# Retention attention with a two-level router: scores on array quarters, router products beside the transposes, ranks behind the scores

## The chip, the cores and the metric

The kernel runs on one core of a Trainium2 chip. The metric is the device time of one execution in microseconds (us). An execution is one launch, from the inputs in the chip's main memory to the finished output there. Five engines work beside one another, each with its own queue of instructions in program order: TensorE (PE, with PEld for its weight loads), VectorE (DVE), ScalarE (ACT), GpSimd (POOL) and SyncE (SP), which here only starts transfers (DMAs).

## The reference

Two stages. The first is a linear attention with a decay for each of 8 heads; q, k and v have 4 sequences of 768 tokens and 64 features a head. The second sends each of the 3072 tokens (512 features) to one of four groups, and in it to one of four experts, of a two-layer network of 1024 hidden features.

```python
for t in range(S):
    state = gamma[None, :, None, None] * state + np.einsum('bhd,bhe->bhde', k[:, :, t], v[:, :, t])
    y[:, :, t] = scale * np.einsum('bhd,bhde->bhe', q[:, :, t], state)
...
g_logits = x @ w_group
g_idx = np.argmax(g_logits, axis=1)
...
        h = np.maximum(xg[mask_e] @ w1[g, e], 0.0)
        ye = h @ w2[g, e]
        combined = g_w[mask_g][mask_e] * e_w[mask_e]
        out[tok_idx] = combined[:, None] * ye
```

g_w and e_w are the softmax weights of the chosen group and of the chosen expert.

## The kernel before

**Attention (lines 856 to 920).** The 3072 tokens are cut into 24 chunks of 128, six to a sequence, and `attention` runs over them (`ch` is the chunk). Inside a chunk the sum over keys is made by products, across chunks by a state. In program order a chunk issues: `vprep(ch+2)` (POOL: v times a power of the decay), `state_out` (L260, query by state, on 64 by 64 quarters of the array), `value_out` (L273, masked scores by values, 128 by 64), `state_mm` (L236, keys by values into the state in PSUM), `out_x` (DVE, L285: the chunk's x, written as `xt` from two PSUM tiles `op`; a chunk takes both, so the next chunk's `state_out` can start only when they are read), `state_copy` (ACT), router steps, the load of q and k of chunk ch+5, `logits(ch-1)`, `keys_mm(ch+1)` (L193, four transposes; the last chunk of a sequence needs none, nor a state), `trans_mm(ch-1)` (L291, four transposes of x) with `x_store(ch-1)` to main memory, `score_mm(ch+2)` (L214), `score_mask(ch+2)` (DVE, L221, one for each half of the heads), more router steps, and `logits_mm(ch)`. The first chunk of a sequence has no `state_out`.

**Scores (L203 to L214).** Heads are in four pairs. For each pair the two heads use the upper and the lower 64 rows of the array at once. The weights are the 128 keys (64 rows by 128 columns), the 128 queries are streamed, and the mask then sets to zero the products of keys later than their query.

**Router logits.** They are made in two steps: `logits_mm` (L305) multiplies each 128-feature quarter of x with its part of the router's weights (20 columns padded to 32, four column strips at once), ACT copies the result (`logits_copy`, `ls`), and `logits` (L316) adds up the four quarters by a product with a 0/1 matrix (`C_SEL`), from where ACT copies 20 columns to `L`. Both results and the ranks below lie in one PSUM tile, `log`.

**Routing (`route`, L324 on).** Chunks are routed in groups: `BATCHES = [(0, 4), (4, 4), (8, 4), (12, 5), (17, 4), (21, 3)]` (first chunk, count). A group's work is a generator, of which `route_steps` takes 5 steps at a time (6 from chunk 16 on), three times a chunk: twelve steps of small DVE operations (m, d, q, m2, o, oh, sm, eg, se, u, w, the reciprocal), then a "wait" mark, then the rank products on TensorE (L387, L389) from `oh`, then r1 and `nb` (DVE reads the ranks), r2, sf and slot. Only the first of the three calls, right behind `out_x` and `state_copy`, passes `ranks=True` and may go past the mark. A group enters the list in the chunk that follows its last one. `enlist` then scatters each chunk's tokens to the experts' lists (`meta`) by POOL; `clear_lists` fills the lists once before.

**Experts 0 and 1.** They have fixed early lists (of the first 12 chunks: `ua`, `va`) and late lists (`ub`, `vb`). The weights of `ua` are loaded in 16 parts in chunks 2 to 17 and split in chunks 4 to 19 (ACT makes the fp16 part `wh`, POOL the rest `wl`, L600 and L601); `va` is loaded in chunks 18 to 21 and its eight splits are made in chunks 20 (0 on DVE, 1 on POOL), 21 (2), 22 (3, 4, 5) and after the attention (6, 7). The layers of `ua` are a generator too, `self.first`: its first 24 products stand ahead of chunk 23's `state_out` (place 0 of `beside`), the others between the steps that follow chunk 23.

**Behind the attention** come the last group's route, the layers of `ua`, the expert order (`order`, small DVE operations on one row), then `va`, `ub`, `vb` and the other 14 experts (`us`, by size), each with transposes of gathered x (`xtrans`, L641), a first layer (`hps`, L664), a second (`yps`, L692, L742, L744) and a scatter of the result (POOL, L795). While one expert is computed, the next one's weights are split on ACT and DVE and those of the one after are loaded on SP's queue.

Of the kernel before, what the change touches and what calls it, by code (L numbers as in the profile page):

```python
# [22 lines left out]
P = 128  # L23
NC = S // P
# [22 lines left out]
C_TRI, C_GV, C_GS, C_SEL = 0, 128, 176, 180  # L47
C_STRI, C_DESC, C_SEG, C_KP, C_WP, C_IT = 200, 328, 348, 367, 386, 405
C_END = C_IT + MAXI

# [10 lines left out]
def constants():  # L61
# [3 lines left out]
    c[:, C_TRI:C_TRI + P] = s[:, None] <= s[None, :]  # L65

    n = np.arange(NC)[None, :, None] * P + s[:, None, None] + 1.0
    c[:, C_GV:C_GV + NC * H] = (g ** -n).reshape(P, NC * H)
    c[:, C_SEL:C_SEL + 20] = s[:, None] % 32 == np.arange(20)[None, :]
# [22 lines left out]
class Kernel:  # L92
# [15 lines left out]
    def setup(self):  # L108
# [15 lines left out]
        self.wr = cp.tile([P, 4, 32], F32, name="wr")  # L124
        nc.vector.memset(self.wr, 0.0)
        nc.sync.dma_start(self.wr[:, :, 0:20], self.a_wr.rearrange("p (k e) -> p k e", k=4))
# [58 lines left out]
    def keys_mm(self, ch):  # L185

        nc, s = self.nc, self.st[ch]
        if ch % NC == NC - 1:
            return
        s["kt"] = kt = self.pp.tile([P, 512], F32, name="kt", tag="big", bufs=3)  # L190
        for p in range(4):
            cs = slice(p * P, p * P + P)
            nc.tensor.transpose(kt[:, cs], s["ld"][:, DM + p * P:DM + p * P + P], self.ident)  # L193

    def keys_copy(self, ch):
        s = self.st[ch]
        if ch % NC == NC - 1:
            return
        s["kk"] = self.vp.tile([P, DM], F32, name="kk", bufs=2)
        self.nc.scalar.activation(s["kk"], s["kt"], AF.Copy)  # L200

    def score_mm(self, ch, pars=(0, 1)):


        nc, pp, s = self.nc, self.pp, self.st[ch]
        qT = s["ld"][:, 0:DM]
        kT = s["ld"][:, DM:2 * DM]
        for par in pars:
            s["sc", par] = pp.tile([P, 512], F32, name="sc", tag="big", bufs=3)
        for p in range(4):  # L210
            for par in pars:
                rs = slice(64 * par, 64 * par + 64)
                cs = slice(p * P, p * P + P)
                nc.tensor.matmul(s["sc", par][:, cs], kT[rs, cs], qT[rs, cs], start=True, stop=True)  # L214

    def score_mask(self, ch, par):
# [3 lines left out]
        tri = self.cst[:, C_TRI:C_TRI + P].unsqueeze(1).broadcast_to([P, 4, P])  # L220
        nc.vector.tensor_tensor(s["pf"][:, par], s["sc", par].rearrange("p (g t) -> p g t", g=4), tri, ALU.mult)  # L221
# [65 lines left out]
    def trans_mm(self, ch):  # L287
        nc, s = self.nc, self.st[ch]
        s["tp"] = self.pp.tile([P, 512], F32, name="tp", tag="tra", bufs=1)
        for j in range(4):  # L290
            nc.tensor.transpose(s["tp"][:, j * P:j * P + P], s["xt"][:, j, :], self.ident)  # L291

# [7 lines left out]
    def logits_mm(self, ch):  # L300

        nc, s = self.nc, self.st[ch]
        s["lt"] = lt = self.log[:, 256 + ch % 2 * P:256 + ch % 2 * P + P]
        for j in range(4):
            nc.tensor.matmul(lt[32 * j:32 * j + 32, :], self.wr[:, j, :], s["xt"][:, j, :], start=True, stop=True)  # L305

    def logits_copy(self, ch):
        s = self.st[ch]
        s["ls"] = self.wp.tile([P, P], F32, name="ls", bufs=2)
        self.nc.scalar.activation(s["ls"], s["lt"], AF.Copy)  # L310

    def logits(self, ch):

        nc, s = self.nc, self.st[ch]
        lg = self.log[:, ch % 2 * 64:ch % 2 * 64 + 20]
        nc.tensor.matmul(lg, s["ls"], self.cst[:, C_SEL:C_SEL + 20], start=True, stop=True)  # L316
# [4 lines left out]
        nc.scalar.activation(self.Ls[i][:, ch - c0, :], lg, AF.Copy)  # L321
# [530 lines left out]
    def attention(self, extra, beside):  # L852
# [20 lines left out]
        for ch in range(NCH):  # L873
# [7 lines left out]
            if ch == 6:  # L881
# [11 lines left out]
            self.route_steps(steps, True)  # L893
            if ch + 5 < NCH:
                self.load(ch + 5)
            if ch >= 1:
                self.logits(ch - 1)
# [3 lines left out]
            if ch >= 1:  # L901
                self.trans_mm(ch - 1)
                self.x_store(ch - 1)
# [9 lines left out]
            self.route_steps(steps)  # L913
# [3 lines left out]
            self.route_steps(steps)  # L917
            self.logits_mm(ch)
            self.logits_copy(ch)
            extra(ch)  # L920

    def route_steps(self, n, ranks=False):
# [4 lines left out]
        for i in range(n):  # L927
            if self.steps:
# [3 lines left out]
                if t == "wait" and not (ranks and i == 0):  # L932
# [3 lines left out]
    def run(self):  # L936
        tc, nc = self.tc, self.nc
        with ExitStack() as ctx:
# [29 lines left out]
            def extra(ch):  # L968
# [4 lines left out]
                if 18 <= ch <= 21:  # L973
                    self.wload(va, ch - 18)
# [3 lines left out]
                if ch == 20:  # L978
                    self.wsplit(va, 0)
                    self.wsplit(va, 1, eng=nc.gpsimd)  # L980
                if ch == 21:
                    self.wsplit(va, 2)
                if ch == NCH - 2:
                    for k in (3, 4, 5):
                        self.wsplit(va, k)
                    self.first = self.layers(ua)

            def beside(ch, place):
# [8 lines left out]
                if ch == NCH - 1 and place == 0:  # L997
                    first(2)
# [9 lines left out]
            first(1)  # L1008
            self.logits(last)
            assert not self.steps  # L1010
# [4 lines left out]
            first(1)  # L1015
            self.trans_mm(last)
            self.x_store(last)
            first(2)
# [38 lines left out]
            for i, k in enumerate(self.layers(ub)):  # L1057
                if k == 3:
# [84 lines left out]
```

## Time and profile before

| | us |
|---|---|
| median of 3 runs | 455.16 |
| lowest, highest | 452.87, 455.31 |
| the profiled execution | 459.31 |
| its span, first to last instruction | 457.6 |

| stretch of the span | PE busy | DVE busy | ACT busy | POOL busy | granted clock |
|---|---|---|---|---|---|
| 40 to 60 us (attention) | 18.88 of 20 | 13.87 | 9.69 | 12.53 | 1.00 |
| 100 to 120 us (attention, fourth group) | 15.72 of 20 | 10.71 | 6.64 | 9.79 | 0.83 |
| 120 to 140 us (last chunks) | 15.32 of 20 | 14.18 | 10.85 | 11.41 | 0.83 |
| 260 to 300 us (experts) | 39.79 of 40 | 31.41 | 24.69 | 15.96 | 1.00 |

The second table is from the view of busy time by windows. In rows of the timeline the columns are the start in us, the length in us, the engine, the line, the operation, the tiles (written <- read), the shape and the count; brackets give the idle time of the engine before it and what ended that. A TensorE row's length reaches to the modelled end of its last product, which overlaps the next row; so blocks are measured from start to start.

### The profile page before, as it was taken

How to read it: one execution, taken by the hardware profiler on the slowest of the kernel's cores; microseconds unless marked ns; L12 is line 12 of the kernel's file. 1: busy time of each engine (PE TensorE's matmuls, PEld its weight loads, DVE VectorE, ACT ScalarE, POOL GpSimd, SP SyncE). 2: the span in 40 equal slices, each digit the busy share in tenths (PEclk: the TensorE clock that was granted, in tenths of full speed). 3: DMA queues.
4: the chain of work that ended last, by engine and by line, in shares of the span. 5: the costliest groups of instructions: out<-in, count | busy, mean ns of one | idle time of the engine just before them, and what ended most of it. 6: DMA issues, size and time to landing. Idle time of an engine off the chain costs nothing.

```text
span 457.6 us, 12943 instructions
## 1 busy us (share of the span) xinstructions
PE 426.9 (93%) x5373; PEld 344.7 (75%) x5404; DVE 296.9 (65%) x499; ACT 233.0 (51%) x391; POOL 173.1 (38%) x148
## 2 busy tenths in 40 slices
PE   7998989987959899899999999999999999999991
PEld 4787878776848676677687978879789788788770
DVE  1448586565477626577679878677687687697720
ACT  1234445442545226455655656657666676676610
POOL 3714666655742622124150615336145044042011
PEclk9999999997988999999999999999999999999996
DMA  7878988885751295747766687787887887877000
GB/s 231 306 253 317 288 262 266 243 279 184 224 181 49 84 386 188 274 155 236 274 229 224 232 287 257 246 288 247 285 295 276 302 258 295 313 279 273 13 27 31
DMA packets 35055, 106.80 MB, mean 233 GB/s; under 512 B 13720, under 2 KB 14360, under 8 KB 27316
## 3 DMA queue, kind: packets, MB, share of 16 engines
q1 hardware_dynamic: 24052, 88.65, 57.3%
q0 software_dynamic: 10944, 17.31, 11.0%
q8 instruction: 43, 0.70, 0.6%
q14 instruction: 16, 0.13, 0.1%
HBM read 93.53 MB, written 13.77 MB: 234 GB/s over the span
## 4 chain that ended last, share of the span: by engine, by line
PE 58%; issue 24%; POOL 8%; DVE 5%; DMA 2%; SPq 1%; ACT 0%; POOLq 0%; DVEq 0%
PE hps L664 20%; PE yps L692 9%; PE yps L742 5%; PE yps L744 5%; PE sc L214 4%; PE op L273 4%; POOL out L795 3%; POOL xg L623 3%; PE tpx L641 2%; PE op L260 2%; PE tp L291 2%; PE kt L193 1%; PE stp L236 1%; PE log L305 1%; DMA ld<-qk 1%
## 5 line engine op out<-in xcount | busy, mean ns | idle before, releaser
L601 DVE TENSOR_TENSOR wl<-wf,wh 128x1024 bf16<-128x1024 f32 x119 | 144.0, 1220 | 40.8 <-ACT wh L600 34.5
L664 PE MATMUL hps<-xbh,wh 128*128 128x128 f16 (+14 forms) x576 | 135.4, 246 | 1.6 <-ACT xbh L643 0.8
L664 PE MATMUL hps<-xbl,wh 128*128 128x128 bf16 (+14 forms) x576 | 135.4, 246 | 1.1 <-issue 0.6
L664 PE MATMUL hps<-xbh,wl 128*128 128x128 f16 (+14 forms) x576 | 135.4, 246 | 0.9 <-issue 0.9
L600 ACT ACTIVATE wh<-wf 128x1024 f16<-128x1024 f32 (+1 forms) x136 | 133.9, 999 | 0.1
L795 POOL DMA_INDIRECT out<-yo,mt x32 | 41.4, 1294 | 192.8 <-ACT yo L760 170.5
L664 PEld LDWEIGHTS <-wh 128*128 128x128 f16 x1152 | 103.4, 98 | 5.7 <-issue 3.1
L669 ACT ACTIVATE hh<-hps 128x256 f16<-128x256 f32 (+14 forms) x72 | 35.0, 488 | 58.9 <-PE hps L664 52.4
L744 PEld LDWEIGHTS <-wh 128*128 128x128 f16 x704 | 44.6, 98 | 21.0
L664 PEld LDWEIGHTS <-wl 128*128 128x128 bf16 x576 | 56.7, 98 | 2.8 <-issue 2.2
L221 DVE TENSOR_TENSOR pf<-sc,cst 128x512 f32<-128x512 f32 x48 | 30.8, 684 | 41.3 <-PE sc L214 40.1
L623 POOL DMA_INDIRECT xg<-xd,mt x32 | 51.8, 1619 | 13.5 <-issue 5.8
L672 DVE SCALAR_TENSOR_TENSOR hl<-hps,hh 128x256 bf16<-128x256 f32 (+14 forms) x70 | 38.5, 552 | 22.5 <-ACT hh L669 21.0
L643 ACT ACTIVATE xbh<-tpx 128x512 f16<-128x512 f32 (+13 forms) x32 | 16.9, 527 | 45.1 <-PE tpx L641 45.0
L425 POOL DMA_INDIRECT meta<-src,slot x24 | 24.5, 1022 | 25.5 <-DVE rows L415 8.9
L644 DVE TENSOR_TENSOR xbl<-tpx,xbh 128x512 bf16<-128x512 f32 (+13 forms) x32 | 19.3, 602 | 22.7 <-ACT xbh L643 22.6
L742 PE MATMUL yps<-wh,hh 128*128 128x512 f16 x88 | 33.4, 380 | 0.0
L742 PE MATMUL yps<-wh,hl 128*128 128x512 f16 x88 | 33.4, 379 | 0.0
L214 PE MATMUL sc<-ld 64*128 64x128 f32 x384 | 30.5, 302 | 1.9 <-DMA ld<-qk 1.9
L601 POOL TENSOR_TENSOR wl<-wf,wh 128x512 bf16<-128x512 f32 (+1 forms) x17 | 20.7, 1220 | 29.7 <-ACT wh L600 26.3
L744 PEld LDWEIGHTS <-wl 128*128 128x128 bf16 x352 | 23.1, 98 | 10.4
L214 PEld LDWEIGHTS sc<-ld 64*128 64x128 f32 x384 | 25.6, 203 | 6.8 <-issue 5.6
(138 smaller groups left out, 658.6 us busy)
## 6 DMA issues: line engine op xcount, KB each, us to landing
wf<-w1p SPq DMA_DIRECT2D x28, 1024.0 KB
wf<-w2p SPq DMA_DIRECT2D x28, 1024.0 KB
ld<-qk SPq DMA_DIRECT2D x23, 512.0 KB
xd<-xr SPq DMA_DIRECT2D x24, 256.0 KB
vt<-vb SPq DMA_DIRECT2D x6, 768.0 KB
wf<-w1p SPq DMA_DIRECT2D x8, 256.0 KB
wf<-w2p SPq DMA_DIRECT2D x8, 256.0 KB
wf<-w1p POOLq DMA_DIRECT2D x2, 1024.0 KB
```

The source lines that it names most:

```text
L214: nc.tensor.matmul(s["sc", par][:, cs], kT[rs, cs], qT[rs, cs], start=True, stop=True)
L221: nc.vector.tensor_tensor(s["pf"][:, par], s["sc", par].rearrange("p (g t) -> p g t", g=4), tri, ALU.mult)
L600: nc.scalar.activation(u["wh"][i][:, cs], u["wf"][i][:, cs], AF.Copy)
L601: (eng or nc.vector).tensor_tensor(u["wl"][i][:, cs], u["wf"][i][:, cs], u["wh"][i][:, cs], ALU.subtract)
L623: nc.gpsimd.indirect_dma_start(out=xg[0:r, i, :], out_offset=None, in_=self.xd[0:n, :], in_offset=bass.IndirectOffsetOnAxis(ap=mt[0:r, i, ...
L664: nc.tensor.matmul(hv[:, a, 0:W], l[:, k, fs], r[:, k, 0:W], start=(n == 0), stop=(n == 11))
L669: nc.scalar.activation(hh[:, f, 0:W], hv[:, :, 0:W], AF.Relu)
L672: nc.vector.scalar_tensor_tensor(*rest)
L692: nc.tensor.matmul(ps[0:r, :], l[:, k, ts], m[k], start=(n == 0), stop=(n == 23))
L742: nc.tensor.matmul(big, h[:, k, 0:P], w[k], start=(n == 0), stop=(n == 23))
L744: nc.tensor.matmul(yv[:, d, 0:r], w[k][:, d * P:d * P + P], h[:, k, P:P + r], start=(n == 0 and d == 0), stop=(n == 23), skip_group_check= ...
L795: s = nc.gpsimd.indirect_dma_start(out=self.out, out_offset=bass.IndirectOffsetOnAxis(ap=mt[0:r, i, 0:1].bitcast(U32), axis=0), in_=yo[0:r ...
```

## The change

Five things are changed.

1. *Scores on quarters.* Each product of 128 keys by 128 queries is cut in two on 64 by 64 quarters: the earlier 64 keys by all 128 queries, and the later 64 keys by the later 64 queries. The quarter of later keys by earlier queries is not computed; the mask's zeros stand over it. Two PSUM tiles, cleared once by DVE, take the scores of all chunks. So that both column halves of the array get as much work, every other pair of heads has its keys in swapped halves (`KEYS`); keys, values, decays and the mask follow in the packing.
2. *Router products.* One step: four products with x as the weights (128 by 128) and the router's 20 columns streamed, added up in PSUM, right behind the transposes of x in `trans_mm`. The copy `ls`, the 0/1 matrix and its product go.
3. *Ranks.* The first call of `route_steps` in a chunk no longer goes past the mark, the two behind the scores and masks do; every mark now ends a call.
4. *Splits and loads.* `clear_lists` stands in chunk 4, the loads of `va` in 17 to 20, its splits 0, 1 and 2 on DVE in 19, 20 and 21; 3 stands ahead of `order`, 4 to 7 behind it. POOL clears the second gather buffer in place of DVE.
5. *Around the end of the attention.* The first 24 products of `ua` stand behind chunk 23. During `vb`, the transposes of the next expert's x stand at steps 8 and 10, its splits at 3, 7, 9, 11 and 13.

```diff
-C_TRI, C_GV, C_GS, C_SEL = 0, 128, 176, 180
+C_TRI, C_GV, C_GS, C_STRI, C_DESC = 0, 256, 304, 308, 436
+KEYS = np.array([np.arange(P) ^ (64 * (h // 2 % 2)) for h in range(H)])
...
+        self.sc = [self.pp.tile([P, 512], F32, name=f"sc{par}", tag="big", bufs=3) for par in range(2)]
+        self.kt = self.pp.tile([P, 512], F32, name="kt", tag="big", bufs=3)
+        for sc in self.sc:
+            nc.vector.memset(sc, 0.0)
...
         for p in range(4):
-            for par in pars:
-                rs = slice(64 * par, 64 * par + 64)
-                cs = slice(p * P, p * P + P)
-                nc.tensor.matmul(s["sc", par][:, cs], kT[rs, cs], qT[rs, cs], start=True, stop=True)
+            for late in range(2):
+                for par in range(2):
+                    half = (late + p) % 2
+                    rs = slice(64 * par, 64 * par + 64)
+                    ks = p * P + 64 * half
+                    cs = slice(p * P + 64 * late, p * P + P)
+                    nc.tensor.matmul(
+                        self.sc[par][64 * half:64 * half + 64, cs], kT[rs, ks:ks + 64], qT[rs, cs],
+                        start=True, stop=True, skip_group_check=True,
+                    )
...
+        for j in range(4):
+            nc.tensor.matmul(self.log[:, 0:20], s["xt"][:, j, :], self.wr[:, j, :], start=(j == 0), stop=(j == 3))
...
-            nc.tensor.matmul(lt[32 * j:32 * j + 32, :], self.wr[:, j, :], s["xt"][:, j, :], start=True, stop=True)
-
-    def logits_copy(self, ch):
-        s = self.st[ch]
-        s["ls"] = self.wp.tile([P, P], F32, name="ls", bufs=2)
-        self.nc.scalar.activation(s["ls"], s["lt"], AF.Copy)
...
-        nc.tensor.matmul(lg, s["ls"], self.cst[:, C_SEL:C_SEL + 20], start=True, stop=True)
...
-            if ch == 6:
+            if ch == 4:
                 self.clear_lists()
...
-            self.route_steps(steps, True)
+            self.route_steps(steps)
...
             if ch >= 1:
                 self.trans_mm(ch - 1)
+                self.logits(ch - 1)
                 self.x_store(ch - 1)
...
-            self.route_steps(steps)
+            self.route_steps(steps, True)
...
-            self.route_steps(steps)
-            self.logits_mm(ch)
-            self.logits_copy(ch)
+            self.route_steps(steps, True)
...
-                if t == "wait" and not (ranks and i == 0):
+                if t == "wait":
                     self.waiting = True
                     break
...
-                if 18 <= ch <= 21:
-                    self.wload(va, ch - 18)
+                if 17 <= ch <= 20:
+                    self.wload(va, ch - 17)
...
-                if ch == 20:
-                    self.wsplit(va, 0)
-                    self.wsplit(va, 1, eng=nc.gpsimd)
-                if ch == 21:
-                    self.wsplit(va, 2)
+                if 19 <= ch <= 21:
+                    self.wsplit(va, ch - 19)
                 if ch == NCH - 2:
-                    for k in (3, 4, 5):
-                        self.wsplit(va, k)
                     self.first = self.layers(ua)
...
-                if ch == NCH - 1 and place == 0:
-                    first(2)
...
-            first(1)
+            first(2)
+            self.trans_mm(last)
             self.logits(last)
+            self.x_store(last)
...
-            first(1)
-            self.trans_mm(last)
-            self.x_store(last)
-            first(2)
+            first(4)
...
+            nc.gpsimd.memset(self.xg[1], 0.0)
+            self.wsplit(va, 3)
             self.steps.append(self.order())
             self.route_steps(99)
             assert not self.steps
-            nc.vector.memset(self.xg[1], 0.0)
-            self.wsplit(va, 6)
-            self.wsplit(va, 7)
+            for k in range(4, 8):
+                self.wsplit(va, k)
...
             for i, k in enumerate(self.layers(vb)):
-                if k in KX:
-                    self.xtrans(us[0], ("tra", "sta")[KX.index(k)], (KX.index(k),))
-                if k is not None and k < 5:
-                    self.wsplit(us[0], k + 3)
-                    if k % 2 == 0:
-                        self.wload(us[1], k // 2 + 1)
+                if i in (8, 10):
+                    self.xtrans(us[0], ("tra", "sta")[i // 2 - 4], (i // 2 - 4,))
+                if i in (3, 7, 9, 11, 13):
+                    j = (3, 7, 9, 11, 13).index(i) + 3
+                    self.wsplit(us[0], j)
+                    if j % 2:
+                        self.wload(us[1], j // 2)
```

More of the change, by code (lines that the diff above doesn't have):

```diff
@@ L64, in constants @@
     c = np.zeros((P, C_END), np.float64)
-    c[:, C_TRI:C_TRI + P] = s[:, None] <= s[None, :]
-    n = np.arange(NC)[None, :, None] * P + s[:, None, None] + 1.0
+    for i in range(2):
+        c[:, C_TRI + i * P:C_TRI + i * P + P] = (s ^ (64 * i))[:, None] <= s[None, :]
+    n = np.arange(NC)[None, :, None] * P + KEYS.T[:, None, :] + 1.0
     c[:, C_GV:C_GV + NC * H] = (g ** -n).reshape(P, NC * H)
-    c[:, C_SEL:C_SEL + 20] = s[:, None] % 32 == np.arange(20)[None, :]
     for half in range(2):
@@ L189, in keys_mm @@
             return
-        s["kt"] = kt = self.pp.tile([P, 512], F32, name="kt", tag="big", bufs=3)
         for p in range(4):
             cs = slice(p * P, p * P + P)
-            nc.tensor.transpose(kt[:, cs], s["ld"][:, DM + p * P:DM + p * P + P], self.ident)
+            nc.tensor.transpose(self.kt[:, cs], s["ld"][:, DM + p * P:DM + p * P + P], self.ident)
     def keys_copy(self, ch):
@@ L219, in score_mask @@
             s["pf"] = self.wp.tile([P, 2, 4, P], F32, name="pf", bufs=3)
-        tri = self.cst[:, C_TRI:C_TRI + P].unsqueeze(1).broadcast_to([P, 4, P])
-        nc.vector.tensor_tensor(s["pf"][:, par], s["sc", par].rearrange("p (g t) -> p g t", g=4), tri, ALU.mult)
+        tri = self.cst[:, C_TRI:C_TRI + 2 * P].unsqueeze(1).broadcast_to([P, 2, 2 * P])
+        o, i = s["pf"][:, par].rearrange("p g t -> p (g t)"), self.sc[par]
+        o, i = (t.rearrange("p (i t) -> p i t", i=2) for t in (o, i))
+        nc.vector.tensor_tensor(o, i, tri, ALU.mult)
     def state_mm(self, ch):
@@ L320, in logits @@
             self.Ls[i] = self.rp.tile([P, BM, 20], F32, name="L", bufs=2)
-        nc.scalar.activation(self.Ls[i][:, ch - c0, :], lg, AF.Copy)
+        self.nc.scalar.activation(self.Ls[i][:, ch - c0, :], self.log[:, 0:20], AF.Copy)
     def route(self, i):
@@ L926, in route_steps @@
         self.waiting = False
-        for i in range(n):
+        for _ in range(n):
             if self.steps:
@@ L1057, in run @@
             for i, k in enumerate(self.layers(ub)):
-                if k == 3:
+                if i == 7:
                     self.xtrans(vb)
@@ L1114, in tokm, with keyed @@
         return a.reshape(B, H, NC, P, D).transpose(0, 2, 3, 1, 4).reshape(B, NC, P, DM)
+    def keyed(a):
+        a = a.reshape(B, H, NC, P, D)
+        return np.stack([a[:, h][:, :, KEYS[h]] for h in range(H)], axis=1).reshape(B, H, S, D)
     rows = np.concatenate([h * D + np.arange(D) for g in HEAD for h in g])
-    qk = np.concatenate([feat(q), feat(k)], axis=3).reshape(NCH, P, 2 * DM)
-    vb = tokm(v).reshape(NCH // GR, GR, P, DM).transpose(0, 2, 1, 3).reshape(NCH // GR, P, GR * DM)
+    qk = np.concatenate([feat(q), feat(keyed(k))], axis=3).reshape(NCH, P, 2 * DM)
+    vb = tokm(keyed(v)).reshape(NCH // GR, GR, P, DM).transpose(0, 2, 1, 3).reshape(NCH // GR, P, GR * DM)
     wr = np.concatenate([inp["moe_w_group"], inp["moe_w_expert"].transpose(1, 0, 2).reshape(DM, NX)], axis=1)
```

23 lines of the change are left out of this document (6 added, 17 removed).

## The prediction, made before the changed kernel was run

> **What bounds the kernel now.** I read the page first: who is busy, and when.
>
> ```profile
> span 457.6 us, 12943 instructions
> PE 426.9 (93%) x5373; PEld 344.7 (75%) x5404; DVE 296.9 (65%) x499; ACT 233.0 (51%) x391; POOL 173.1 (38%) x148
> ```
>
> TensorE is the bound. So time can be won in two ways: less TensorE work, or fewer of its gaps. Next the timeline of TensorE for one chunk of the attention stage; columns are start, length, line, tiles, count.
>
> ```profile
> 49.51 1.16 PE L214 MATMUL sc<-ld 64*128 64x128 f32 x16
> 50.60 0.42 PE L305 MATMUL log<-xt,wr 128*32 128x128 f32 x8
> 50.96 0.67 PE L260 MATMUL op<-ld,V 64*64 64x128 f32 x16
> 51.55 1.09 PE L273 MATMUL op<-pf,vs 128*64 128x128 f32 x16
> 52.48 0.64 PE L236 MATMUL stp<-vs,kk 128*64 128x64 f32 x16
> 53.04 0.40 PE L316 MATMUL log<-cst,ls 128*128 128x20 f32 x2
> 53.29 0.63 PE L193 MATMUL kt<-ident,ld 128*128 128x128 f32 x4
> 53.76 0.60 PE L291 MATMUL tp<-ident,xt 128*128 128x128 f32 x4
> 54.29 0.38 PE L214 MATMUL sc<-ld 64*128 64x128 f32 x2
> ```
>
> One chunk takes 54.29 - 49.51 = 4.78 us with TensorE never waiting. Start to start, the blocks cost: scores 1.09, router products 0.36, state output 0.59, value output 0.93, state 0.56, router sum 0.25, key transposes 0.47, x transposes 0.53. Then the same timeline where it does wait, at the fourth and fifth routing group.
>
> ```profile
> 17.32 1.09 PE L273 MATMUL op<-pf,vs 128*64 128x128 f32 x16
> ...
> 96.30 1.09 PE L273 MATMUL op<-pf,vs 128*64 128x128 f32 x16
> ...
> 100.02 1.09 PE L273 MATMUL op<-pf,vs 128*64 128x128 f32 x16
> ...
> 105.20 0.71 DVE L285 TENSOR_TENSOR xt<-op,gx 128x256 f32<-128x256 f32 x2
> ...
> 106.19 0.62 PE L316 MATMUL log<-cst,ls 128*128 128x20 f32 x2 [3.04 <-DVE nb L397]
> ```
>
> ```profile
> 124.67 1.16 PE L214 MATMUL sc<-ld 64*128 64x128 f32 x16
> 126.75 1.09 PE L273 MATMUL op<-pf,vs 128*64 128x128 f32 x16
> ...
> 132.73 0.40 PE L316 MATMUL log<-cst,ls 128*128 128x20 f32 x2 [2.75 <-DVE nb L397]
> ...
> 139.81 1.14 PE L273 MATMUL op<-pf,vs 128*64 128x128 f32 x16
> ```
>
> From value output 1 (17.32) to value output 22 (126.75) pass 109.4 us. Without waits it would be 15 full chunks of 4.78, three of 4.34 (the next chunk is a sequence's last, without the 0.47 of key transposes, less 0.03 that this had hidden) and three of 100.02 - 96.30 = 3.72 at the change of sequence: 95.9 us. So **13.5 us are waits**. The last step, 22 to 23, takes 13.06 us. I then asked for the windows around these gaps, cut where the granted clock changes (columns: window, length, PE busy, PEld, DVE, ACT, POOL, granted clock, DMA share, GB/s).
>
> ```profile
> 102.41:105.81 3.40, 0.34 (x6) 0.25 (x6) 3.23 (x10) 0.46 (x2) 2.16 (x2) 1.00 0.67 181
> 105.82:112.64 6.82, 6.45 (x54) 5.18 (x56) 2.21 (x8) 2.18 (x5) 2.44 (x3) 0.50 0.42 126
> 126.30:129.71 3.41, 2.04 (x49) 1.73 (x46) 3.24 (x11) 1.05 (x3) 1.79 (x2) 1.00 0.91 276
> 129.72:133.12 3.40, 0.65 (x9) 0.55 (x9) 3.22 (x13) 0.70 (x2) 0.00 (x0) 1.00 0.50 201
> 133.13:139.94 6.81, 6.25 (x58) 4.88 (x59) 4.03 (x5) 4.88 (x8) 4.33 (x4) 0.50 0.11 39
> ```
>
> A window with 0.34 or 0.65 us of work is followed by half clock, for 6.8 us, two windows of 3.41; one with 2.04 us is not. A drop costs up to 6.83 / 2 = 3.4 us. In these gaps DVE is busy (3.23, 3.22): it works through the routing group's small operations, and TensorE stands behind it.
>
> **The change part by part.** *Scores.* The value output has eight pair passes of 128 columns and one 64-column weight load in 0.93, about 0.11 a pass; the state's 64-column passes come to 0.06 (0.56 less about 0.09 for the change of array shape that follows; an estimate). So the scores' 1.09 are eight passes (0.88), a 128-column load (0.11) and a change of shape. Afterwards each quarter passes four times 128 and four times 64 columns, 6/8 of 0.88 = 0.66, plus 0.06 for the shorter load; the state output has the same 64 by 64 shape, so no change of shape lies between, and its own first load is hidden: 0.72 in place of 1.09, and 0.53 in place of 0.59. Bounds: 0.66, if all loads hide; 0.95, if quarters of unequal length wait for each other and nothing of the 0.88 is won. I take 0.72, since the state output already runs four quarters beside one another (16 in 0.59). The mask reads as many elements as before; two PSUM clears on DVE lie ahead of the first load of q and k, for which TensorE waits.
>
> *Router.* The 0.36 of L305 and the 0.25 of L316 go; the key transposes show 0.03 of a load that L316 had covered. Added are four float32 products with 128-column weights and 20 columns. L316 is such a product.
>
> ```profile
> 53.04 0.19 PEld L316 LDWEIGHTS log<-cst,ls 128*128 128x128 f32 x1
> 53.15 0.19 PEld L316 LDWEIGHTS log<-cst,ls 128*128 128x128 f32 x1
> 53.18 0.22 PEld L193 LDWEIGHTS kt<-ident,ld 128*128 128x128 f32 x1
> ```
>
> Its first load holds the array for 53.15 - 53.04 = 0.11. Eight at 0.11, the first under the last transpose, are 0.78. If the second load of a product were as quick as 53.18 - 53.15 = 0.03 suggests, it would be 4 x 0.14 - 0.11 = 0.45; if no load is hidden and each product costs all of L316's 0.25, 1.0. I take 0.78: L193's load may have been queued early. They keep the shape of the transposes, so no change of shape is added. ScalarE loses one copy a chunk.
>
> Per chunk: -0.37 - 0.36 - 0.06 - 0.25 + 0.03 + 0.78 = **-0.23**. Over the 18 steps with a state output it gives -4.1, at the three changes of sequence (no state output, so that a change of shape stays) -0.07 each: -4.4 together.
>
> A rule speaks against this. The Trainium skill, page "TensorE: Matmul & The Clock Gate", Part 3, has weight loads overlap running products only in another row group, and products start in program order. By it the router's loads would all show and the sum per chunk would be about nothing. The trace disagrees for the loads: the key transposes, all in one row group, come 0.11 apart with loads of their own; no run here shows unequal quarters.
>
> *Ranks.* Here lies most of the waiting. The rank products move behind the scores, and the next router products come after the next transposes, over 3 us of TensorE work later; by then DVE has read the ranks (its r and nb come straight after the masks). So the waits for nb go, the two quoted above among them. What is late next is xt. Ten to twelve routing operations stay on DVE ahead of the next xt. The timeline of DVE and TensorE for the second group:
>
> ```profile
> 60.45 0.74 DVE L285 TENSOR_TENSOR xt<-op,gx 128x256 f32<-128x256 f32 x2
> ...
> 61.01 0.65 PE L305 MATMUL log<-xt,wr 128*32 128x128 f32 x8 [0.78 <-DVE xt L285]
> ```
>
> Before, L305 waited there; now the next state output does, since its two PSUM tiles come free with xt. The scores of that step ended at 54.29 + 1.09 - 0.09 = 55.29, so xt, for which L305 waited until 61.01, is done some 5.7 later. TensorE gets there after 4.78 - 0.23 = 4.55: a gap of about 1.2, in which the rank products hide (their oh is done before xt). Behind the waiting state output stands all of TensorE in order, and DVE's next masks with it; POOL's list scatters, which wait for the slots, move by half a chunk (earlier for the first three groups, later for the next) and have until chunk 17, where they are needed. Three groups: 3.6 us. For the fourth group, xt ends at 105.20 + 0.71 = 105.91. Its scores had ended 0.45 before value output 18 (100.02; L305 and a change of shape lie between), so xt comes 6.35 after them. TensorE's work until then, a first chunk without state output, is 4.2: a gap of 2.15. Waits of 5.75 in place of 13.5: **-7.8**.
>
> *The last step.* The scores of 23 ended at 124.67 + 1.09 - 0.09 = 125.67.
>
> ```profile
> 131.72 0.75 DVE L285 TENSOR_TENSOR xt<-op,gx 128x256 f32<-128x256 f32 x2
> ```
>
> xt(22) ended at 132.47, 6.8 later, behind the routing and a split that stays in this place. TensorE has 3.9 us of work after those scores (0.53 + 0.93 + 0.56 + 0.49 + 0.78 + 0.44 for the transposes of ua, 0.15 of ranks), waits 2.9, then does the state output: value output 23 at +7.4, that is 6.9 after value output 22 in place of 13.06: **-6.2**. Price: the 24 products that filled the gap come behind it, and two router blocks lie there without scores to win anything (0.78 each, against 0.36 and 0.25). The chain has such a run of 24:
>
> ```profile
> 144.20 1.34 PE hps L664 x24
> ```
>
> That is 1.34 + 2 x 0.17, and some 0.2 of late loads: **+1.9**. The last routing group starts as much later as TensorE has more to do, so the late lists keep their slack.
>
> *Splits and queues.* Chunks 19 to 21 get 1.22 us of DVE each, with masks 1.29 and xt 0.86 under 4.55: hidden; without that cover up to 1 us a chunk. Three splits (3.50 on DVE at chunk 22) no longer stand ahead of xt(23); five instead of two follow the lists' order, 3.7 us more ahead of hl of va, which three PSUM buffers and the 1.9 us cover. I take 0, bounds -1 and +2. The clear of xg moves from DVE (0.91) to POOL, which idles there. The loads of va go to SP's queue one chunk earlier, behind the same x stores; buffers are free. The list clear (1.08 on POOL) stands two chunks earlier, ahead of every scatter: 0. In vb, the second transposes of us[0] come before its last products:
>
> ```profile
> 189.39 0.27 PE L664 MATMUL hps<-xbh,wh 128*128 128x256 f16 x1 [0.83 <-ACT xbh L643]
> ```
>
> That wait goes: **-0.8**. The loads of us[1] start some 3 us later, with 20 us to spare. Behind 189 us TensorE is full, so all shifts with it.
>
> Sum without a clock drop: -4.4 - 7.8 - 6.2 + 1.9 - 0.8 = **-17.3 us**.
>
> *Clock.* The gaps of 1.2 leave 2.2 us in a window, more than the 2.04 that passed. The gap of 2.9 leaves 0.5 to 1.9, by where the windows fall; 2.15 leaves 1.3 or more, between the two kinds seen. I take one drop, 3.0 us: **-14.3**.
>
> **To the time.** The profiled execution took 459.31 us (its span 457.6), the median of the three runs is 455.16. From the first I get 445.0, from the second 440.9. The runs to be compared are like the median's, so I take **441.0**.
>
> **Rivals.** *No drop*: 455.16 - 17.3, about 438. For it: both drops seen followed gaps near 3 us in one window. Against: 0.65 us of work did not save one. The Trainium skill, page "TensorE: Matmul & The Clock Gate", Part 1, asks for an idle window of about 3.4 us, by which a gap of 2.9 would cause no drop; the window with 0.65 speaks against so strict a reading. *Two drops*: 444. *Dearer products*: unequal quarters wait (+0.2 a chunk) or the router's loads show (+0.22): 21 to 23 chunks, +4 to +5, 446. *Drop at every group*, the other side: the router block streams only 20 columns a product, so it may count as idle; with a 1.2 gap beside it, 2.2 - 0.7 = 1.5 us of work remain. If all five groups drop for two windows, 17 us are lost and the time is 455, no change; for three windows each (5.1), 25.6 are lost: 463, slower. It decides where a group costs over 4 us. Against it: after both drops full clock returned in two windows.
>
> **How the numbers follow.** One drop 0.38; none 0.24; two 0.12; dearer products 0.17; every group 0.09 (0.05 no change, 0.04 slower). Half a per cent, 2.3 us, is what a measurement can tell from none: faster 0.91, same 0.05, slower 0.04. The range of 8 in 10 goes from 433 (the router at 0.45 gives -0.33 a chunk) to 450 (dearer products with two drops).
>
> **What would show it.** Chunks without waits at 4.55; router products at 0.78 behind the transposes; no wait for nb, but state output waiting on xt, 1.2 for three groups, 2.2 and 2.9 for two; value output 23 near 121. A chunk at 4.78 or gaps above 3 us would make it wrong.

## The result, and the profile after

| | before | after |
|---|---|---|
| median, us | 454.5 | 442.25 |
| lowest, highest | 452.87, 455.31 | 440.45, 442.88 |
| the profiled execution | 459.31 | 442.88 |
| its span | 457.6 | 441.2 |

The medians are of four runs each, before among them run again. The ratio of after to before is **0.973** (95% interval 0.969 to 0.977): faster. The forecast was 441.0, with a range of 433 to 450. The head of the page of after:

```profile
span 441.2 us, 13629 instructions
PE 420.0 (95%) x5740; PEld 348.7 (79%) x5740; DVE 294.4 (67%) x500; ACT 227.8 (52%) x367; POOL 176.0 (40%) x148
```

TensorE's share rises from 93 to 95%: the span lost 16.4 us, of which only 6.9 (426.9 to 420.0) were busy time. The timeline of TensorE, a chunk that does not wait and then the second group's:

```profile
49.87 0.90 PE L219 MATMUL sc<-ld 64*64 64x128 f32 x32
50.59 0.62 PE L270 MATMUL op<-ld,V 64*64 64x128 f32 x16
51.13 1.09 PE L283 MATMUL op<-pf,vs 128*64 128x128 f32 x16
...
53.12 0.60 PE L301 MATMUL tp<-ident,xt 128*128 128x128 f32 x4
53.55 0.97 PE L303 MATMUL log<-wr,xt 128*128 128x20 f32 x8
54.45 0.90 PE L219 MATMUL sc<-ld 64*64 64x128 f32 x32
...
55.32 0.26 PE L386 MATMUL log<-oh,ones 128*128 128x64 bf16 x4
56.12 0.99 PE L270 MATMUL op<-ld,V 64*64 64x128 f32 x16 [0.55 <-DVE xt L295]
57.05 1.09 PE L283 MATMUL op<-pf,vs 128*64 128x128 f32 x16
```

One chunk takes 54.45 - 49.87 = 4.58 us. The next value output comes 57.05 - 51.13 = 5.92 after the last: a gap of 1.33, in which the state output (L270) waits for xt. What DVE and POOL did then:

```profile
53.53 1.18 POOL L598 TENSOR_TENSOR wl<-wf,wh 128x512 bf16<-128x512 f32 x1 [2.11 <-ACT wh L597]
54.68 1.03 POOL L174 TENSOR_TENSOR vs<-vt,cst 128x512 f32<-128x512 f32 x1
```

```profile
53.88 0.87 DVE L368 TENSOR_TENSOR eg<-sm,o 128x16 f32<-128x16 f32 x1
54.78 0.17 DVE L371 TENSOR_REDUCE se<-eg 128x4 f32<-128x16 f32 x1
54.87 0.88 DVE L374 TENSOR_SCALAR u<-sm 128x4 f32<-128x4 f32 x1
55.66 0.74 DVE L295 TENSOR_TENSOR xt<-op,gx 128x256 f32<-128x256 f32 x2
```

The routing operations run right up to xt, and two of them, 16 and 4 elements long, take 0.87 and 0.88 us: each ends with the POOL operation beside it (54.71 and 55.71). The end of the attention:

```profile
114.41 1.09 PE L283 MATMUL op<-pf,vs 128*64 128x128 f32 x16 [1.35 <-POOL vs L174]
...
120.13 0.99 PE L270 MATMUL op<-ld,V 64*64 64x128 f32 x16 [2.17 <-DVE xt L295]
121.05 1.28 PE L283 MATMUL op<-pf,vs 128*64 128x128 f32 x16
```

Two gaps are left, 1.4 and 2.3 us. TensorE's waits for nb are gone from the view of waits, which for TensorE now opens with L270:

```profile
PE op L270 <- DVE xt L295: 3.7, 4, 2.2
```

By windows (columns as in the prediction), the larger gap is followed by half clock:

```profile
118.41:121.82 3.41, 1.69 (x30) 1.38 (x32) 3.32 (x11) 0.14 (x1) 0.00 (x0) 1.00 0.20 77
121.83:128.66 6.83, 6.83 (x50) 6.50 (x46) 1.28 (x6) 1.06 (x3) 3.95 (x4) 0.50 0.11 39
```

Cut at the value outputs of chunks 1, 22 and 23 and at the first product of us[0] (each read from the timeline), the two profiled executions compare like this:

| stretch, us | before | after |
|---|---|---|
| start to value output 1 | 17.3 | 14.5 |
| value output 1 to 22 | 109.4 | 99.9 |
| value output 22 to 23 | 13.1 | 6.6 |
| value output 23 to us[0] | 49.6 | 52.8 |
| us[0] to the end | 268.2 | 267.3 |

The profiled execution of before (459.31) is slower than all four timed runs of before, so the two spans lie further apart than the medians.

### The profile page after: what moved, and what is told of

It is laid out like the page before. It is cut to its first block, busy times and chain, and to the rows that moved or that the text cites. A ratio compares the mean times of both kernels' runs of the same rounds, so it can differ in the third digit from the quotient of the medians.

```text
span 441.2 us, 13629 instructions
## 1 busy us (share of the span) xinstructions
PE 420.0 (95%) x5740; PEld 348.7 (79%) x5740; DVE 294.4 (67%) x500; ACT 227.8 (52%) x367; POOL 176.0 (40%) x148
## 4 chain that ended last, share of the span: by engine, by line
PE 58%; issue 21%; POOL 7%; DVE 7%; DMA 4%; SPq 1%; POOLq 0%; ACT 0%; DVEq 0%
PE hps L661 20%; PE yps L689 8%; PE yps L739 6%; PE yps L741 4%; PE op L283 4%; POOL out L792 3%; PE log L303 3%; PE sc L219 3%; POOL xg L620 3%; DMA meta<-src,slot 2%; PE op L270 2%; PE tp L301 2%; PE tpx L638 2%; PE kt L197 2%; PE stp L246 1%
## 5 line engine op out<-in xcount | busy, mean ns | idle before, releaser
L598 DVE TENSOR_TENSOR wl<-wf,wh 128x1024 bf16<-128x1024 f32 x120 | 146.2, 1228 | 40.2 <-ACT wh L597 40.0
L620 POOL DMA_INDIRECT xg<-xd,mt x32 | 54.2, 1693 | 17.2 <-DMA mt<-meta 7.9
L422 POOL DMA_INDIRECT meta<-src,slot x24 | 25.6, 1067 | 29.0 <-DVE slot L404 12.2
L739 PE MATMUL yps<-wl,hh 128*128 128x512 bf16 x88 | 33.4, 379 | 0.0
L174 POOL TENSOR_TENSOR vs<-vt,cst 128x512 f32<-128x512 f32 x24 | 25.0, 1043 | 10.1 <-DMA vt<-vb 9.4
L283 PE MATMUL op<-pf,vs 128*64 128x128 f32 x384 | 26.4, 280 | 2.4 <-POOL vs L174 1.3
```

The costliest lines, as they stand in the source:

```text
L283: nc.tensor.matmul(s["o"][par][64 * half:64 * half + 64, pp * P:pp * P + P], s["vs"][:, hs], s["pf"][:, par, p, :], start=(c == 0 and pp = ...
L598: (eng or nc.vector).tensor_tensor(u["wl"][i][:, cs], u["wf"][i][:, cs], u["wh"][i][:, cs], ALU.subtract)
L620: nc.gpsimd.indirect_dma_start(out=xg[0:r, i, :], out_offset=None, in_=self.xd[0:n, :], in_offset=bass.IndirectOffsetOnAxis(ap=mt[0:r, i, ...
L739: nc.tensor.matmul(big, h[:, k, 0:P], w[k], start=(n == 0), stop=(n == 23))
```

## The experiments

All times are device us, ratios are to runs of the kernel before on the same chip. The runs r1 to r4 were on a chip where before took 458.48, the others where it took 454.3 to 454.6; so ratios are compared across them.

| run | what it is | median | ratio (interval) | 1 to 22 | 22 to 23 | 23 to us[0] |
|---|---|---|---|---|---|---|
| r5 | after, again | 443.0 | 0.974 (0.970 to 0.977) | 100.1 | 7.0 | 50.8 |
| r1 | before, ranks moved | 462.1 | 1.003 (1.000 to 1.007) | 115.4 | 10.8 | 49.5 |
| r2 | after, old router | 457.3 | 0.997 (0.995 to 1.000) | 113.6 | 7.3 | 51.0 |
| r6 | after, old ranks | 456.0 | 0.999 (0.995 to 1.003) | 110.2 | 9.5 | 50.4 |
| r3 | after, quarter computed | 449.1 | 0.979 (0.975 to 0.982) | 104.8 | 7.0 | 51.4 |
| r4 | after, old scores | 448.8 | 0.978 (0.975 to 0.981) | 105.2 | 6.9 | 51.8 |
| r8 | after, steps spread | 436.4 | 0.963 (0.960 to 0.966) | 95.5 | 5.4 | 49.6 |
| r11 | before, steps spread | 452.4 | 0.997 (0.994 to 1.001) | 108.8 | 9.5 | 48.4 |
| r9 | r8, two splits on POOL | 436.5 | 0.959 (0.956 to 0.963) | 96.5 | 5.4 | 49.7 |
| r7 | after, gap filled | 445.6 | 0.980 (0.977 to 0.983) | 100.3 | 9.5 | 49.5 |
| r10 | after, old splits | 442.5 | 0.975 (0.971 to 0.979) | 98.9 | 9.6 | 48.8 |
| r12 | after, old vb | 444.1 | 0.976 (0.972 to 0.980) | 100.3 | 6.7 | 52.1 |

My theory of the gain: less work in the scores, and waits for nb that go because the ranks move behind the scores and the router behind the x transposes. The rivals: one of these does it all, or the queue on DVE is the only cause.

**The measure, r5.**

> The changed kernel itself, beside a run of before on the same chip, as the measure for the runs that are sent with it. Both theories: 442 us, ratio 0.97.

443.0, as expected. Its profile differs from that of after mainly in two places: it starts 2.1 us later (value output 1 at 16.65) with half clock from 10.29 to 13.70, and half clock behind the last gap lasts 3.41 us, not 6.83:

```profile
122.93:126.34 3.41, 3.41 (x33) 2.75 (x32) 2.04 (x8) 0.00 (x0) 1.57 (x2) 0.50 0.01 0
```

**Is it the ranks, the router, or both? r1, r2 and r6.** In r1 only the calls of the routing steps change:

```diff
-            self.route_steps(steps, True)
+            self.route_steps(steps)
...
-            self.route_steps(steps)
+            self.route_steps(steps, True)
```

> The kernel before with the ranks moved behind the scores and nothing else. Theory A (the move of the ranks alone takes the waits for nb away): four groups lose 2 us or so each and the last step some 4 us: 443 to 447 us, and no wait for nb is left but state output waits for xt. Theory B (it works only together with the router's products behind the transposes, since the router products at the chunk's end, L305, share the PSUM tile log with the ranks that now stand just ahead of them): L305 waits for nb, 1 to 2.5 us a group; 450 to 455 us.

r1 leaves part of the work out: its first list scatter (POOL, at 43.9 us) now comes ahead of the clearing of the lists in chunk 6 (46.7), so the first chunk's tokens leave the lists (from us[0] to the end it still takes 268.2 us, as before does). r2 takes the opposite way:

```diff
-        for j in range(4):
-            nc.tensor.matmul(self.log[:, 0:20], s["xt"][:, j, :], self.wr[:, j, :], start=(j == 0), stop=(j == 3))
...
+            self.logits_mm(ch)
+            self.logits_copy(ch)
             extra(ch)
```

> The changed kernel with the two-step router put back in its old places. By work alone: the new products cost 0.90 us a chunk start to start, the old two steps 0.36 and 0.25 less 0.03, so 24 x 0.3 = 7 us less, 435 us (with my predicted sizes 24 x 0.2 = 5, 437). Rival: L305 stands right behind the ranks in the tile log and waits for nb, and the last two chunks make no gain; then the work saved is given back in waits: 441 to 447 us, with waits for nb at L305.

And r6 keeps the new router and lets only the first of the three calls pass the mark again:

```diff
-            self.route_steps(steps)
+            self.route_steps(steps, True)
...
-                if t == "wait":
+                if t == "wait" and not (ranks and i == 0):
```

> The changed kernel with the ranks back in the first call of a chunk (behind x, before the key transposes), the router's products left beside the x transposes. Theory A (the pair is needed: ranks behind the scores and router behind the transposes): the router's products, 0.9 us behind the ranks in the same tile, wait for nb again, 1 to 2 us for each of five groups: 447 to 451 us. Theory B (the router's new place alone takes the waits away, the ranks could have stayed): 441 to 444 us.

All three end where before is, with the waits that theory B of r1, the rival of r2 and theory A of r6 name. r2 and r6 cost more than those two forecasts: behind their gaps half clock lasts 17.1 us in each, in r5 3.4, and the forecasts left that out. The views of waits, before, r1, r2 and r6:

```profile
PE log L316 <- DVE nb L397: 7.2, 5, 3.0
```

```profile
PE log L305 <- DVE nb L397: 12.4, 5, 2.6
```

```profile
PE log L318 <- DVE nb L410: 12.5, 5, 2.8
```

```profile
PE log L303 <- DVE nb L394: 7.6, 5, 2.3
PE log L384 <- DVE oh L356: 3.7, 2, 2.6
```

In r2 the second group looks like this (L402 ranks, L318 the router's first products, L234 the mask):

```profile
59.32 0.26 PE L402 MATMUL log<-oh,ones 128*128 128x64 bf16 x4
...
60.79 1.25 DVE L234 TENSOR_TENSOR pf<-sc,cst 128x512 f32<-128x512 f32 x2
62.10 0.16 DVE L410 TENSOR_TENSOR nb<-log,nb 128x16 f32<-128x16 f32 x1
...
62.31 0.42 PE L318 MATMUL log<-xt,wr 128*32 128x128 f32 x8 [2.74 <-DVE nb L410]
```

The ranks are written at 59.3, but DVE reads them behind the masks, at 62; the router's products, which use the same PSUM tile `log`, stand directly behind the ranks and wait. The waits change their place, and their sum stays: in before, TensorE's waits from 20 to 145 us for nb (7.2), oh (2.6), xt (2.3) and `ls` (0.4) make 12.5 us; those for nb alone make 12.4 in r1 and 12.5 in r2. So neither move does it alone: **most of the gain is the distance in TensorE's order between the ranks and the next product into their tile**, and it takes both moves. The ranks and the router's products lie in different columns of `log`, so what they share is the tile; a tile of their own for the ranks was not tried. In r6 the distance is short on the other side, and the ranks wait for oh as well.

In work r2 saves little: without waits its chunk takes 4.52 us, 0.06 less than after's, not 0.2 to 0.3, since its x transposes take 0.53 in place of 0.44 and its scores 0.83 in place of 0.72; I put that down to the array's shape, which changes behind both of them in r2. Its waits leave windows of 0.55 to 1.02 us of work, each followed by half clock, five times 3.41 us.

**The scores, r3 and r4.** r3:

```diff
-                    cs = slice(p * P + 64 * late, p * P + P)
+                    cs = slice(p * P, p * P + P)
```

> The changed kernel with the skipped quarter of the scores computed as well: the later keys take all 128 queries too, so each quarter streams eight times 128 columns. Theory A (columns streamed are what is won; unequal quarters run beside one another): the scores' block goes from 0.72 to 0.94, 24 x 0.22 = 5 us, less about 1 us where the chunk waits for xt anyway: 446 to 447 us. Theory B (only the change of shape was won, the shorter quarters wait for the longer): block stays at 0.72, 442 us.

r4 puts one product of 128 keys by 128 queries in place of the two:

```diff
+            for par in range(2):
+                rs = slice(64 * par, 64 * par + 64)
+                cs = slice(p * P, p * P + P)
+                nc.tensor.matmul(self.sc[par][:, cs], kT[rs, cs], qT[rs, cs], start=True, stop=True)
```

> The changed kernel with the scores as products of 128 keys by 128 queries again (keys and mask packed as after). Theory A: the block goes from 0.72 to 1.09 and the state output from 0.55 to 0.59, 24 x 0.41 = 10 us, less about 2 us where five groups wait for xt anyway: 450 us. Rival: DVE sets the pace in more chunks than the waits show, and TensorE's time in the scores is covered for half: 445 to 447 us.

The scores and the state output behind them, r3 and then r4:

```profile
48.14 1.10 PE L219 MATMUL sc<-ld 64*64 64x128 f32 x32
49.07 0.62 PE L270 MATMUL op<-ld,V 64*64 64x128 f32 x16
```

```profile
48.12 1.16 PE L216 MATMUL sc<-ld 64*128 64x128 f32 x16
49.21 0.67 PE L264 MATMUL op<-ld,V 64*64 64x128 f32 x16
```

The block is 0.93 in r3 and 1.09 in r4, against 0.72 in after: theory A in both, as far as the block goes. Of the gain of 0.37, 0.21 is columns not streamed; the other 0.16 is what parts r4 from r3, shorter weight loads and a change of shape less, which no run takes apart. Chunks without waits take 4.79 and 5.00, so after saves 0.21 and 0.42 in each; but 1 to 22 differs by only 4.7 and 5.1 from r5, where 21 steps of 0.42 would be 8.8. In r4 a longer chunk fills gaps: where the groups wait, its step is 5.72, in after 5.92. By the ratios the old scores cost 0.5% (2 us), by the traces 5; the runs do not settle which. Both ratios make about 445 us of r5's before, less than theory A gave (446 to 447, and 450); r4 is nearest to its rival (445 to 447).

**The queue on DVE, r8 and r11.** One line in each, in after (r8) and in before (r11):

```diff
-            steps = 6 if late else 5
+            steps = 4 if late else 3
```

> The changed kernel with 3 routing steps a call (4 from chunk 16 on) in place of 5 (6). Theory A (state output waits for x because ten to twelve routing operations stand ahead of it on DVE): three gaps of 1.33 us go, the one of the fourth group loses about 1 us, the last 1 us: 436 us, and 433 if the clock drop goes with the last gap. Rival: the same operations only come in more chunks and make x late there too, by 0.5 us in two chunks a group: 439 to 441 us.

> The kernel before with 3 routing steps a call (4 from chunk 16 on), the ranks where they were. Theory A (all the waits come from DVE standing late; where the ranks stand matters little): the nb waits shrink to under 1 us each: 443 to 447 us. Theory B (the ranks behind x, with the router's sum 0 us of other work behind them in the same tile, cost a round trip through DVE whatever its queue holds): nb waits of 1.5 us or more in each of five groups stay, and the last step stays long: 449 to 453 us.

r8 is the fastest kernel but for r9, which stands level with it: 436.4 where its neighbour r5 took 443.0, as theory A had it. The same group and TensorE's longest waits from 20 us on, r8:

```profile
58.02 0.26 PE L386 MATMUL log<-oh,ones 128*128 128x64 bf16 x4
58.21 0.67 PE L270 MATMUL op<-ld,V 64*64 64x128 f32 x16
```

```profile
PE hps L661 <- DVE hl L669: 1.4, 1, 1.4
PE stp L246 <- issue: 0.8, 1, 0.8
```

The state output follows the ranks without a wait; no wait for xt is left, and no half clock before 424 us. Against r5: 4.6 us less from 1 to 22, 1.7 from 22 to 23, 1.2 behind; about 1.7 of this is r5's half clock. The same line in before wins nothing that can be told: waits for nb of 6.7 us in five groups and for xt of 1.9 remain (theory B, with 1.3 a group where it had 1.5), and three windows behind the waits fall to half clock. Here spreading pays only once the ranks are out of the way.

**Filling the last gap, r7.** The first 24 products of `ua` return ahead of chunk 23's state output:

```diff
+                if ch == NCH - 1 and place == 0:
+                    first(2)
...
-            first(4)
+            first(2)
```

> The changed kernel with 24 of the products of ua back ahead of chunk 23's state output (24 fewer between the last x transposes and the ranks of the last group). Theory A (the gap of 2.3 us there makes the clock drop that follows, and both can be had back): gap 0.6 us, no window of half clock near 122 us, 3 to 5 us less: 437 to 439 us. Rival: the products are only moved; the wait comes back at the ranks of the last group, which had 48 products ahead of them and now have 24, and the drop with it: 441 to 443 us.

Neither: there is no gain, and the median is 2.6 above r5's, with intervals that just touch. TensorE and DVE at that place:

```profile
123.70 0.22 PE L661 MATMUL hps<-xbl,wh 128*128 128x128 bf16 x1 [2.13 <-DVE xbl L641]
```

```profile
122.31 0.75 DVE L295 TENSOR_TENSOR xt<-op,gx 128x256 f32<-128x256 f32 x2
122.97 0.68 DVE L641 TENSOR_TENSOR xbl<-tpx,xbh 128x512 bf16<-128x512 f32 x1
```

The products wait for xbl, which DVE makes behind xt: what was to fill the gap stands in the same queue, one place later.

**The splits, r10 and r9.** r10 restores the old chunks:

```diff
-                if 19 <= ch <= 21:
-                    self.wsplit(va, ch - 19)
+                if ch == 20:
+                    self.wsplit(va, 0)
+                    self.wsplit(va, 1, eng=nc.gpsimd)
+                if ch == 21:
+                    self.wsplit(va, 2)
                 if ch == NCH - 2:
+                    for k in (3, 4, 5):
+                        self.wsplit(va, k)
...
-            for k in range(4, 8):
+            for k in range(6, 8):
```

> The changed kernel with the loads of va and its splits back in their old chunks (loads 18 to 21, splits 20 to 22 and two after the attention). Predicted: 0, bounds -1 and +2, so 441 to 444 us. Theory A (the three splits of chunk 22 stand ahead of x of chunk 23 on DVE): the x transposes of chunk 23 come 1 to 2 us late behind the 24 products of ua, but hl of va comes 3.7 us earlier and its wait of 1.4 us goes: 442 to 444 us. Rival (a split spread out is worth something in the fourth and fifth group): 445 us or more.

442.5: nothing, as the sum of two effects that cancel. 22 to 23 takes 9.6 in place of 7.0, not for the reason of theory A alone: ahead of xt of chunk 22, DVE's first routing operation (L338) takes 3.25 us beside POOL's split and `vs`, and 0.48 in r5. But value output 22 does not wait for POOL, and va's first 96 products take 5.36 us, in r5 6.90, since hl is not late. r9 sets out from r8:

```diff
+                if ch == NCH - 2:
+                    self.wsplit(va, 3, eng=nc.gpsimd)
+                    self.wsplit(va, 4, eng=nc.gpsimd)
...
-            self.wsplit(va, 3)
...
-            for k in range(4, 8):
+            for k in range(5, 8):
```

> The kernel of r8 with the splits 3 and 4 of va made in chunk 22 on POOL, which idles there for 6 us. Theory A (five splits on DVE behind the expert order make hl of va late, so that va's first layer waits 1.4 us): the wait goes, 1.4 us less than r8, ratio 0.960. Rival: POOL's splits make DVE's small operations beside them slower (one took 1.92 us beside POOL's vs, 0.24 elsewhere) and delay the list scatters: no gain, ratio 0.963 to 0.966.

The wait for hl goes, and another of the same size comes:

```profile
118.89 4.21 POOL L598 TENSOR_TENSOR wl<-wf,wh 128x1024 bf16<-128x1024 f32 x2 [4.36 <-ACT wh L597]
119.00 2.10 DVE L398 TENSOR_TENSOR r<-r,oh 128x64 f32<-128x64 f32 x1
...
121.38 1.74 DVE L404 CAST slot<-sf 128x4 uint32<-128x4 f32 x1
...
123.59 0.68 PE L301 MATMUL tp<-ident,xt 128*128 128x128 f32 x4 [1.42 <-DVE xt L295]
```

L398 and L404 took 0.22 and 0.17 in r8; beside POOL's two splits they end with them, and xt of chunk 23 stands behind. The stretch 23 to us[0] is unchanged (49.7 to 49.6): the rival, by its mechanism. The ratio of 0.959 is the one that theory A gave, but its interval and that of r8 (0.963) overlap.

**The steps of vb, r12.** The transposes and splits of us[0] return to their old steps:

```diff
-                if i in (8, 10):
+                if k in KX:
...
-                if i in (3, 7, 9, 11, 13):
+                if k is not None and k < 5:
```

> The changed kernel with the transposes and splits of the next expert's x during vb at their old steps. Predicted term: the wait of 0.8 us of us[0]'s first layer for its transposes comes back, 443 us, with that row in the trace. Rival: the splits at new steps cost as much elsewhere, 442 us.

```profile
175.52 0.27 PE L661 MATMUL hps<-xbh,wh 128*128 128x256 f16 x1 [0.83 <-ACT xbh L640]
176.24 0.27 PE L661 MATMUL hps<-xbl,wh 128*128 128x256 bf16 x1 [0.46 <-DVE xbl L641]
```

Both waits are there, 1.29 us together; 23 to us[0] is 1.3 longer than in r5, of which about 0.3 is half clock that in r5 lies ahead of value output 23. The medians differ by 1.1, within their intervals.

## Why the prediction was right, and where it was not

| step | predicted | measured |
|---|---|---|
| chunk without waits | 4.55 | 4.58 |
| scores, state output | 0.72, 0.53 | 0.72, 0.54 |
| x transposes and router | 0.53 + 0.78 = 1.31 | 0.43 + 0.90 = 1.33 |
| gaps of three groups | 1.2 each | 1.33 each |
| gap of the fourth | 2.15 | 2.3 |
| value output 1 to 22 | 97.2 | 99.9 |
| gap of the last step | 2.9 | 2.2, and 1.4 ahead of value output 22 |
| value output 22 to 23 | 6.9 | 6.6 |
| wait of us[0] | -0.8 | -1.3 (r12) |
| splits and queues | 0 | 0 in sum (r10) |
| clock drop | 3.0 | about 3.4 (after), 1.7 (r5) |

**Work and waits.** The scores hold to the hundredth, and r3 and r4 show by themselves the two sizes of which they were made up. That waits for xt take the place of those for nb, with 1.2 for three groups, was read off the DVE queue of before, and is what the trace shows. That row had more in it than the prediction names: two of the operations ahead of xt (L368 and L374 in after) are stretched beside POOL, by 1.4 us together in each of the three gaps. The reason given, that the router's products come over 3 us of TensorE work behind the ranks, is what r2 and r6 test: with either move undone the gain is gone.

**Where the steps missed.** From 1 to 22 the sum was 2.7 us too good. The step that failed is "Splits and queues ... I take 0": value output 22 waits 1.35 us for `vs` from POOL. The splits of `va` that now stand on DVE in chunks 19 and 20 hold up a list scatter (L422) and a gather (L620) ahead of it:

```profile
104.84 1.71 DVE L598 TENSOR_TENSOR wl<-wf,wh 128x1024 bf16<-128x1024 f32 x1
105.62 1.81 POOL L422 DMA_INDIRECT meta<-src,slot  x1 [0.17 <-PE stp L246]
...
109.31 1.69 DVE L598 TENSOR_TENSOR wl<-wf,wh 128x1024 bf16<-128x1024 f32 x1
110.07 1.87 POOL L620 DMA_INDIRECT xg<-xd,mt  x1 [0.16 <-issue]
...
113.30 1.05 POOL L174 TENSOR_TENSOR vs<-vt,cst 128x512 f32<-128x512 f32 x1
```

In r10, with the splits and loads of `va` in their old chunks, TensorE is as early (value output 21 at 108.61, in after at 108.41), and it does not wait. There the scatter took 1.01 us, and the gather and `vs` were:

```profile
109.46 1.05 POOL L620 DMA_INDIRECT xg<-xd,mt  x1 [0.16 <-issue]
...
111.87 1.05 POOL L174 TENSOR_TENSOR vs<-vt,cst 128x512 f32<-128x512 f32 x1
```

The two operations that were held up make 1.6 us, by which `vs` comes later in after. The prediction priced a split by DVE's own 1.22 us, which are hidden, and not by what it does to POOL. The delay went on: beside the next scatter and the late `vs`, one of the routing operations ahead of xt of chunk 22 took 1.92 us, in r8 0.24:

```profile
114.85 1.92 DVE L347 SCALAR_TENSOR_TENSOR q<-d,cst 128x80 f32<-128x80 f32 x1
```

So chunk 23's state output starts 7.7 us after the end of its scores, where 6.8 was predicted. That 22 to 23 still came out near 6.9 is luck: value output 22 was late by 1.4 itself.

The rest of the 2.7 is the gaps, 0.13 each, and 0.03 a chunk. In the fourth gap the size came out right by luck: xt accounts for about 1.2 of it, and 1.07 is a stall inside the state products, which the trace puts down to "issue"; r8, where nothing waits for xt, has one of 0.8 too. Its cause was not tested.

**The tail.** The +1.9 for the 24 products did not come: without half clock (r8) the stretch from value output 23 to us[0] takes 49.6 as in before. What r10 and r12 show is +1.5 for hl and -1.3 for us[0]. r7, with the 24 products ahead of value output 23 again, is about 0.7 shorter there than r5 once half the length of half clock is taken off both (48.8 and 49.5, an estimate); the rest was not taken apart.

**The clock.** One drop was right, its cost depends on whether one window or two fall. Half clock in 10.24 to 13.65 of before's profile is missing in after's and present in r5's; after and r5 are the same kernel, so it belongs to the execution. Between these two the start differs by 2.1 us, of which 3.41 us at half clock account for at most 1.7. So of the 16.4 us between the two profiled spans some 2 are no part of the change, and the medians' 12.2 are the better figure. From the median, the predicted -14.3 was 2 us too much, near the 2.7 above.

**The rivals.** No drop: not so, half clock follows the last gap in after and in r5. Dearer products: not seen. The scores' block grows by 0.21 in r3, when the short quarters are filled up, so unequal quarters run beside one another; and the x transposes and the router take 1.33 together, as forecast. Two drops and a drop at every group: not in after, where the smaller gaps left about 2.05 us of work or more in a window; but in r1 and r2, with gaps up to 2.6 and 2.8, all five groups do drop, so the mechanism is real and decides from a longer gap than 1.33.

## What to carry to other kernels

Where another engine must read a result before the next product may write the same PSUM tile, count the TensorE work between the two products: moving one of them alone only moves the wait. When work moves into another engine's free time, look at what runs beside it: here splits on DVE held up POOL's gathers, and through them TensorE. Fill a gap only with work whose inputs do not come from the queue that causes the gap. A long list of small operations is best spread so thin that no call of it reaches the next operation TensorE needs; here that gave 6.6 us beyond the change's 12 (r8), but nothing that can be told where the order was the old one (r11).

## What the runs showed of the hardware

**The clock.** In all fourteen traces I cut the time between 14 and 200 us into the windows of 3.41 us that the drops mark out. Of the windows at full clock, 21 held up to 1.60 us of TensorE's busy time, and half clock followed each; of seven with 1.64 to 1.99, four were followed by it; of those with 2.0 or more none. Two rows of the middle, r6 and r9, of which the first alone was followed by half clock:

```profile
62.65:66.05 3.40, 1.99 (x52) 1.96 (x56) 1.95 (x9) 0.88 (x3) 1.01 (x1) 1.00 0.78 283
```

```profile
120.30:123.70 3.40, 1.98 (x30) 1.83 (x30) 3.33 (x6) 1.06 (x3) 3.10 (x3) 1.00 0.20 77
```

So 2.0 us of work in a window kept the clock in these traces. A gap of 1.33 leaves 2.08 in its window if TensorE works through the rest of it; one of 2.3 leaves 1.1 where it falls into one window. The Trainium skill, page "TensorE: Matmul & The Clock Gate", Part 1, gives the window as 3413 ns and free-running, which the traces bear out: in before the drops start 28.0 and 8.0 windows apart, and in r5 the last gap of the attention comes 2.7 us later than in after, the drop behind it 1.1. It lets the clock fall after an idle window, and these windows were up to 58% busy.

**DVE beside POOL.** Small DVE operations took 0.87, 0.88, 1.74, 1.92 and 2.10 us in place of about 0.2, each ending with a POOL operation. The Trainium skill, page "SBUF — State Buffer", section "Who interferes with whom", has a port pair that the two engines lock for a whole instruction, and DVE reductions that never contend for it; the reductions between them (L371, 0.17) agree. In each of the three gaps of 1.33 two such operations are stretched by 1.4 us together; no run takes POOL's work away there, so that the gaps would close without it is not shown.

**POOL beside DVE.** It goes the other way too. In the first 125 us of the fourteen traces, 255 of POOL's list scatters and gathers began while DVE made no split, and none took over 1.2 us. Another 21 began during a split: each ended 0.9 to 1.0 us behind the end of that split, and 18 of them took 1.4 to 2.0 us.
